# First batch of an induced-attention and leaky-FFN kernel: maxima in three steps, values products moved behind later scores, weight loads spread anew among x

## The chip, the cores and the metric

One core of one Trainium2 chip. The metric is the device time in microseconds of one execution; the kernel before took 1542.71 us, the median of 3 runs.

## What is computed

x is 4 batches of 12480 rows of 128 values, the inducing set is 32 rows of 128, and the FFN has 2048 hidden columns.

```python
def mab(q, kv):
    s = scale * (q @ kv.transpose(0, 2, 1))
    s = s - s.max(-1, keepdims=True)
    a = np.exp(s)
    a /= a.sum(-1, keepdims=True) + 1e-09
    return a @ kv
h = mab(I, x)            # per batch: 32 inducing rows look at all rows of x
y = mab(x, h)            # every row of x looks at the 32 rows of h
...
h = y @ w_in
g = np.maximum(0.01 * h, h)
return (g @ w_out).astype(np.float32)
```

w_in and w_out come as 64-bit floats and are turned to 32-bit on the chip. h of a batch is needed before anything else of that batch can be computed, since the weights that the FFN really uses are h times w_in (tile `hws`).

## The kernel before, in words

Rows of a batch are cut into six groups of 2048 (four blocks of 512, sixteen 128-row slices) and a remainder of 192 rows (group RG). A group comes in as four quarters of 256 KB (tile `xr`).

**First attention, batch 0** (`first_batch`, lines 502 to 597). Nothing can hide it, so it has an order of its own, written out by hand. Per group: `turn` transposes the quarters on PE into PSUM (`xT_ps`, L538) and copies them out on ACT (L544); `scores` multiplies by the inducing rows (`s_ps`, L305); `running` on DVE copies the scores out with their maximum (L317) and spreads it on a diagonal (`rd`, L329), PE adds that up so that every partition has all maxima (`mx_ps`, L334), DVE takes the least of the negated maxima (`nm`, L342 or L345), ACT forms the correction `al` of the older groups (L353) and the exponentials with their sum (L357). `transposed` turns the exponentials on DVE (`ay`, L453), `accumulate` multiplies them with the raw rows on PE (`h_ps`, L425) and adds the result to the running `hacc` times `al` (L441). So the maximum runs on in seven steps, one for each group, and the values products of a group come two rounds later, between the transposes and the scores of a newer group. `sums` (L483) and `normalise` (L496, L498) end it with `hT`.

**Weights.** Eight blocks of 512 KB, four of w_in and four of w_out, each loaded by SP (L179, L185) and converted by `from_double`: one ACT operation (`cv_a`, L131), four DVE operations (`cv_b` L132, `cv_a` L136, `cv_b` L140, `cv_t` L144) and one on POOL (L148). Five loads stand in SP's queue among the quarters of x, behind quarters 2, 6, 10, 14 and 18 (counted from 0); the others follow as buffers come free. Conversion steps (`late`), turns of w_in (`turning`, L233), splits of w_out into a rounded and a remaining part (`splits`, w_hi L202 on ACT, w_lo L203 on POOL) and a small product that keeps PE at work (`keep_ps`, L248) are stepped between the pieces of the first attention by the tables ROUNDS and DRAIN, where "l", "t", "s" and "k" name them. The four w_in blocks are converted first, then the four of w_out.

**From hT on.** The first two tiles of 512 rows take a quick way (`quick`, L739 to L781: q_ps, a_ps, tile A). `expand_weights` makes `hws` in four blocks (product L617, split into two parts L601 and L603). The FFN runs in slots (tile, one of 16 hidden blocks): `ffn_first` makes ph (L821), ghi on ACT (L829) and glo on DVE (L831), and `ffn_second` three output products (L849). The first two tiles share the slots by turns of four. `setup_w12` multiplies turned w_in with w_out (`w_ps`, L259; L263, L265), and `expand_linear` makes from it `m2s` (m_ps, L648), with which a tile ends (L855). `second` is the second attention of the next tiles, `first_scores` and `after_h` the first attention of the next batch, one step at a time among the slots. The main loop (L953) steps each of these lists in a fixed order; every engine carries out its own instructions in the order in which the program issues them.

Of the kernel before, what the change touches and what calls it, by code (L numbers as in the profile page):

```python
# [9 lines left out]
F32 = mybir.dt.float32  # L10
F32R = mybir.dt.float32r
I32 = mybir.dt.int32
# [7 lines left out]
def induced_attention_then_leaky_ffn(  # L20
# [34 lines left out]
    while N - base >= 4 * TOK:  # L55
# [13 lines left out]
    LOADS = [2, 6, 10, 14, 18]  # L69

    ROUNDS = [
        ["", "", "", "", "l"],
        ["l", "l", "", "", "ll", "", ""],
        *[["l", "l", "", "", "ll", "", "", ""]] * 3,
        ["l", "l", "", "", "llt", "", "", ""],
        ["l", "st", "l", "l", "l"],
    ]
    DRAIN = ["l", "", "tk", "l", "l", "", "kk", "", "s"]  # L80

# [36 lines left out]
    def from_double(raw, dst):  # L118
# [7 lines left out]
        n = dst.shape[1]  # L126
# [21 lines left out]
        nc.gpsimd.tensor_tensor(out=dst, in0=a.bitcast(F32), in1=tail, op=ALU.add)  # L148
# [25 lines left out]
    raws = []  # L174

    def load_w_in(c):
        tag, bufs = ("xc", 3) if c < 3 else ("hws", 2)
        raw = sb.tile([P, TOK, 2], I32, tag=tag, name="raw", bufs=bufs)
        nc.sync.dma_start(raw, words(w_in)[:, c * TOK : (c + 1) * TOK, :])  # L179
        return raw  # L180

    def load_w_out(c):
        tag, bufs = ("xc", 3) if c else ("hws", 2)
        raw = sb.tile([P, 4, P, 2], I32, tag=tag, name="raw", bufs=bufs)
        nc.sync.dma_start(  # L185
            raw,
            words(w_out).rearrange("(f p) n t -> p f n t", p=P)[:, 4 * c : 4 * c + 4],
        )
        return raw.rearrange("p f n t -> p (f n) t")

    def setup_w_in():
        for c in range(NF // 4):
            yield from from_double(raws[c], w_in_sb[:, c * TOK : (c + 1) * TOK])
            if c < 3:
                raws.append(load_w_out(c + 1))
            yield

    wraws = []
# [8 lines left out]
    def setup_w_out():  # L207
        for c in range(NF // 4):
            wraw = sb.tile([P, 4, P], F32, tag="xr", name="wraw", bufs=XR)
            wraws.append(wraw)  # L210
            yield from from_double(raws[NF // 4 + c], wraw.rearrange("p f e -> p (f e)"))
            ready.append(c)
            yield

    ready = []

    def parts_of_w_out():
        for c in range(NF // 4):
            while c >= len(ready):
                yield  # L220
            if c:
                yield from idle(3)
            split_w_out(c)
            yield
# [3 lines left out]
    def turn_w_in():  # L228
# [12 lines left out]
        for c in range(NF // 4):  # L241
            copied(turned(c))
            yield
# [7 lines left out]
    def setup_w12():  # L251
        for c in range(NF // 4):
            while c >= len(ready):
                yield
            if c == len(ready) - 1:
                yield from idle(3)
# [245 lines left out]
    def first_batch():  # L502


        order = [*range(RG), RG]
        kinds = [("xr", XR)] * XR + [("ghi", LOOK + 2)] * (LOOK + 2) + [("glo", LOOK + 2)] * (LOOK + 2)
        todo = quarters(0, order)
        for i, (b, g, q) in enumerate(todo):
# [6 lines left out]
            if i in LOADS:  # L515
                c = LOADS.index(i)
                raws.append(load_w_in(c) if c < NF // 4 else load_w_out(0))

        chains, ays = {}, {}
        hacc = None  # L520

        def turn(i, q):
            g = order[i]
# [20 lines left out]
            nc.scalar.copy(  # L544
# [4 lines left out]
        def scores(i):  # L549
            g = order[i]  # L550
            sp = aux_ps("s1_ps")
            for j in range(GROUPS[g][1]):
                columns_product(sp, indT, 0, g, j)
            chains[i] = running(0, g, sp)
            next(chains[i])

        def parts(i):
            return max(1, GROUPS[order[i]][2] // 4) if i < len(order) else 0

        n = len(order)  # L560
        for i in range(n):
            bg = iter(ROUNDS[i])
            for q in range(parts(i)):
                turn(i, q)
                yield next(bg)
            if i >= 1:
                for _ in range(3):
                    next(chains[i - 1])
                yield next(bg)
            if i == n - 1:  # L570
                scores(i)
                yield next(bg)
            if i >= 2:
                hacc = yield from accumulate(0, order[i - 2], hacc, *ays.pop(i - 2), False)
                yield next(bg)
            if i >= 1:
                drain(chains[i - 1])
                ays[i - 1] = transposed(0, order[i - 1])
                yield next(bg)
            if i < n - 1:  # L580
                scores(i)
                yield next(bg)
        bg = iter(DRAIN)
        for _ in range(3):
            next(chains[n - 1])
            yield next(bg)
        hacc = yield from accumulate(0, order[n - 2], hacc, *ays.pop(n - 2), False)
        yield next(bg)
        drain(chains[n - 1])
        ays[n - 1] = transposed(0, order[n - 1])  # L590
        yield next(bg)
        scale = sums(0)
        yield next(bg)
        hacc = yield from accumulate(0, order[n - 1], hacc, *ays.pop(n - 1), False)
        yield next(bg)
        for _ in normalise(0, hacc, scale):
            yield next(bg)
# [424 lines left out]
```

## Time and profile before

| what | value |
| --- | --- |
| median of 3 runs (lowest, highest) | 1542.71 us (1540.13, 1543.12) |
| the profiled execution, its own time | 1541.18 us |
| its span, first to last instruction | 1539.1 us |
| mean granted TensorE clock | 0.992 |
| TensorE busy | 1516.9 us, 99% |
| VectorE busy | 1274.4 us, 83% |
| ScalarE busy | 1005.2 us, 65% |

The profile names the engines PE (TensorE), PEld (its weight loads), DVE (VectorE), ACT (ScalarE), POOL (GpSimd) and SP (SyncE, which issues the DMAs). A row of a timeline has the start in us, the duration, the engine, the line, the operation, what it writes and reads, how often it stands in a row, and in brackets how long the engine was idle before it and what released it. A row of a table by stretches has the stretch and its length, then the busy time of each engine with its number of instructions, then the granted clock (1.00 is full speed), the share of time in which DMA engines were busy, and GB/s. A row of the chain of waits has a start, a duration and the work. Matmuls are pipelined, so the durations of consecutive ones overlap.

### The profile page before, as it was taken

How to read it: one execution, taken by the hardware profiler on the slowest of the kernel's cores; microseconds unless marked ns; L12 is line 12 of the kernel's file. 1: busy time of each engine (PE TensorE's matmuls, PEld its weight loads, DVE VectorE, ACT ScalarE, POOL GpSimd, SP SyncE). 2: the span in 40 equal slices, each digit the busy share in tenths (PEclk: the TensorE clock that was granted, in tenths of full speed). 3: DMA queues.
4: the chain of work that ended last, by engine and by line, in shares of the span. 5: the costliest groups of instructions: out<-in, count | busy, mean ns of one | idle time of the engine just before them, and what ended most of it. 6: DMA issues, size and time to landing. Idle time of an engine off the chain costs nothing.

```text
span 1539.1 us, 22589 instructions
## 1 busy us (share of the span) xinstructions
PE 1516.9 (99%) x7965; PEld 1270.4 (83%) x7965; DVE 1274.4 (83%) x2245; ACT 1005.2 (65%) x1770; POOL 99.0 (6%) x100
## 2 busy tenths in 40 slices
PE   7799999999999999999999999999999999999998
PEld 5588888888888888888888888888888898888887
DVE  6688888887888888888888888887888888888886
ACT  6366666666666666666666666666666666666665
POOL 2110100000101000000001000000111000000000
PEclk9799999999999999999999999999999999999999
DMA  8143334343224354441324246432312112112211
GB/s 277 17 86 59 65 58 90 84 100 69 66 38 86 61 109 93 90 100 22 69 46 90 49 78 129 98 75 50 74 18 51 28 33 49 36 34 42 43 26 21
DMA packets 401313, 104.21 MB, mean 68 GB/s; under 512 B 372368, under 2 KB 374832, under 8 KB 401200
## 3 DMA queue, kind: packets, MB, share of 16 engines
q1 hardware_dynamic: 401152, 102.75, 32.3%
q8 instruction: 63, 1.03, 0.3%
q14 instruction: 50, 0.41, 0.1%
q10 hardware_dynamic: 48, 0.02, 0.0%
HBM read 48.94 MB, written 25.56 MB: 48 GB/s over the span
## 4 chain that ended last, share of the span: by engine, by line
PE 96%; DVE 2%; ACT 1%; DMA 0%; issue 0%; SPq 0%; DVEq 0%
PE po L849 65%; PE ph L821 23%; PE s_ps L305 3%; PE po L855 2%; PE h_ps L425 1%; DMA xr<-in_x_dram 0%; DVE glo L831 0%; PE xT_ps L538 0%; ACT ghi L829 0%; PE a_ps L770 0%; DVE cv_t L144 0%; DVE cv_a L136 0%; PE q_ps L745 0%; ACT xT L544 0%; DVE ay L453 0%
## 5 line engine op out<-in xcount | busy, mean ns | idle before, releaser
L829 ACT ACTIVATE ghi<-ph 128x512 fp32r<-128x512 f32 (+1 forms) x1568 | 929.1, 595 | 492.8 <-PE ph L821 488.0
L831 DVE SCALAR_TENSOR_TENSOR glo<-ph,ghi 128x512 fp32r<-128x512 f32 (+1 forms) x1568 | 1034.1, 678 | 232.0 <-ACT ghi L829 207.7
L821 PE MATMUL ph<-A,hws 128*128 128x512 f32 (+1 forms) x1600 | 607.4, 383 | 5.2 <-DVE hws L603 2.8
L849 PE MATMUL po<-ghi,w_hi 128*128 128x512 f32 (+1 forms) x1568 | 594.2, 379 | 0.0
L849 PE MATMUL po<-glo,w_hi 128*128 128x512 f32 (+1 forms) x1568 | 593.4, 378 | 0.0
L849 PE MATMUL po<-ghi,w_lo 128*128 128x512 f32 (+1 forms) x1568 | 593.4, 378 | 0.0
L821 PEld LDWEIGHTS ph<-A,hws 128*128 128x128 f32 x1600 | 302.5, 189 | 75.8 <-DVE glo L831 21.4
L849 PEld LDWEIGHTS po<-ghi,w_hi 128*128 128x128 f32 x1568 | 297.3, 190 | 43.5 <-issue 0.7
L849 PEld LDWEIGHTS po<-glo,w_hi 128*128 128x128 f32 x1568 | 296.9, 189 | 40.7
L849 PEld LDWEIGHTS po<-ghi,w_lo 128*128 128x128 f32 x1568 | 296.8, 189 | 40.7
L720 POOL TENSOR_TENSOR alo<-aT,ahi 128x512 fp32r<-128x512 f32 x24 | 30.7, 1279 | 669.3 <-ACT ahi L715 666.9
L865 DVE STREAM_TRANSPOSE osb<-po 128x512 f32<-128x512 f32 (+1 forms) x98 | 68.9, 703 | 1.5 <-PE po L855 1.5
L675 POOL TENSOR_TENSOR y<-y,mx 128x512 f32<-128x512 f32 (+1 forms) x27 | 25.3, 936 | 430.4 <-DVE mx L673 430.4
L406 DVE STREAM_TRANSPOSE xT<-xc 128x512 f32<-128x512 f32 x72 | 50.3, 699 | 0.0
L855 PE MATMUL po<-A,m2s 128*128 128x512 f32 (+1 forms) x100 | 43.2, 436 | 0.0
L689 POOL TENSOR_TENSOR y<-y,sm 128x512 f32<-128x512 f32 (+1 forms) x27 | 25.3, 937 | 175.4 <-DVE sm L687 164.2
L425 PEld LDWEIGHTS h_ps<-xr,ay 128*32 128x32 f32 (+1 forms) x784 | 22.7, 112 | 14.2 <-issue 14.2
L425 PE MATMUL h_ps<-xr,ay 128*32 128x128 f32 (+1 forms) x784 | 28.3, 280 | 1.8 <-DVE ay L453 1.8
L305 PE MATMUL s_ps<-xT,indT 128*32 128x512 f32 x192 | 26.4, 622 | 1.1 <-ACT xT L544 1.1
L305 PE MATMUL s_ps<-xT,hT 128*32 128x512 f32 x192 | 25.6, 605 | 0.0
L317 DVE TENSOR_SCALAR_CACHE_REDUCE e<-s_ps 128x512 f32<-128x512 f32 (+1 forms) x28 | 17.1, 609 | 9.3 <-PE s_ps L305 9.2
L855 PEld LDWEIGHTS po<-A,m2s 128*128 128x128 f32 x100 | 18.9, 189 | 2.6
(111 smaller groups left out, 399.8 us busy)
## 6 DMA issues: line engine op xcount, KB each, us to landing
xr<-in_x_dram SPq DMA_DIRECT2D x96, 256.0 KB, 4.4
out_dram<-osb SPq DMA_DIRECT2D x384, 64.0 KB, 2.2
xc<-in_x_dram SPq DMA_DIRECT2D x288, 64.0 KB, 2.7
A<-ahi SPq DMA_DIRECT2D x188, 64.0 KB, 2.0
A<-alo SPq DMA_DIRECT2D x188, 64.0 KB, 2.0
raw<-in_moe_w_in_dram SPq DMA_DIRECT2D x4, 512.0 KB, 6.8
raw<-in_moe_w_out_dram SPq DMA_DIRECT2D x4, 512.0 KB, 7.0
hws<-hwhi SPq DMA_DIRECT2D x24, 64.0 KB, 2.0
```

The costliest lines, as they stand in the source:

```text
L305: nc.tensor.matmul(dst, lhsT, rhs, start=True, stop=True)
L406: nc.vector.transpose(t[:, j, :], blk.rearrange("p n c -> p (n c)"))
L425: nc.tensor.matmul(hp[32 * k : 32 * k + 32, :C], ay[:rows, 4 * q + k, :], xb[:rows, k, :], start=(q == 0), stop=(4 * q + 4 >= K), tile_pos ...
L675: eng.tensor_tensor(out=yv, in0=yv, in1=mx[:rows, :K].unsqueeze(2).broadcast_to([rows, K, M]), op=ALU.subtract,)
L689: eng.tensor_tensor(out=yv, in0=yv, in1=smv.unsqueeze(2).broadcast_to([rows, K, M]), op=ALU.mult)
L720: (eng or nc.gpsimd).tensor_tensor(out=alo[sl], in0=aT.pop((b, g))[: 32 * J, :], in1=ahi[sl].bitcast(F32), op=ALU.subtract,)
L821: nc.tensor.matmul(ph[:, o : o + w], hw[b][1][:, f * P : (f + 1) * P], woven(A4[t][:, o : o + w], t), start=True, stop=True,)
L829: nc.scalar.activation(ghi[:, :n], ph[:, :n], AF.Relu)
L831: nc.vector.scalar_tensor_tensor(out=glo[:, :n], in0=ph[:, :n], scalar=0.0, in1=ghi[:, :n].bitcast(F32), op0=ALU.max, op1=ALU.subtract,)
L849: nc.tensor.matmul(po[:, :n], w[:, f, :], woven(r[:, :n], t), start=(f == 0 and r is ghi and w is w_hi), stop=False)
L855: nc.tensor.matmul(po[:, o : o + w], hw[b][2], woven(a4[:, o : o + w], t, 2), start=False, stop=(o + w == n),)
L865: nc.vector.transpose(osb[:, :n], po[:, :n])
```

## The change

All of it concerns batch 0, the weights and the first two tiles; the code of later batches and the steady slots stays.

- The maximum is taken in three steps: groups 0 to 2, groups 3 and 4, then group 5 with RG. Each step has one `mx_ps` product and one minimum; the values products of a step's groups add up in PSUM (`hpA`, `hpB`, `hpC`), and `hacc` is corrected once for each step. RG comes before the last full group in the order of loads.
- The values products of a group come behind the scores of a later one.
- Weights are loaded in the order w_in 0, w_out 0, w_in 1, w_out 1 and so on, behind quarters 5, 11, 17 of x and the rest behind the last, and converted in that order. The last load waits for the conversion of the fifth block.
- The order of the first attention is written out as one list of calls instead of tables; `l()` is a conversion step. The second quarter is copied on DVE. `keep_ps` is not called any more.
- Uses of a weight block wait, as the program is written out, until the steps that convert it have been issued. In the main loop a conversion step comes in every slot, not every second, and the first slots of the second tile are begun later.

```diff
-    LOADS = [2, 6, 10, 14, 18]
...
+    LOADS = {5: 1, 11: 1, 17: 1, 24: 4}
+    WEIGHTS = [("in", 0), ("out", 0), ("in", 1), ("out", 1), ("in", 2), ("out", 2), ("in", 3), ("out", 3)]
...
+    def convert_weights():
+        for i, (kind, c) in enumerate(WEIGHTS):
+            if kind == "in":
+                yield from from_double(raws[i], lambda: w_in_sb[:, c * TOK : (c + 1) * TOK])
+            else:
+                yield from from_double(raws[i], w_out_part)
+            ready[kind] += 1
+            if i == 4:
+                load_weights()
+            yield
...
         for c in range(NF // 4):
+            while c >= ready["in"]:
+                yield
             copied(turned(c))
             yield
...
+        def peak(g, rd, i):
...
+            nc.vector.tensor_scalar(
+                out=e[:rows, :w], in0=scored.pop(g)[:rows, :w], scalar1=1.0, scalar2=None,
+                op0=ALU.mult, op1=ALU.max, accum_out=rm[:rows],
+            )
...
+            nc.vector.tensor_scalar(
+                out=rd[:, 4 * i : 4 * i + 4], in0=own, scalar1=rm, scalar2=None, op0=ALU.mult,
+                op1=ALU.min, accum_out=any_,
+            )
...
+        turn(3, 0)
+        turn(3, 1)
+        peak(2, rdA, 2)
+        pm = spread(rdA)
+        turn(3, 2)
+        turn(3, 3)
+        nmA, _ = least_of(pm, None)
+        l()
+        exps(0, nmA)
+        scores(3)
+        l()
+        turned(0)
+        hpA = values_ps()
+        values(0, hpA, True, ())
+        exps(1, nmA)
+        peak(3, rdB, 0)
...
+        exps(3, nmB)
+        l()
+        turn(5, 2)
+        turn(RG, 0)
+        turn(5, 3)
+        l()
+        turned(3)
+        exps(4, nmB)
+        l()
+        rdC = peaks(2)
+        scores(5)
+        scores(RG)
+        step(lane["turn"])
+        l()
+        peak(5, rdC, 0)
+        peak(RG, rdC, 1)
+        pm = spread(rdC)
+        hpB = values_ps()
+        values(3, hpB, True, ())
+        turned(4)
+        values(4, hpB, False, range(4))
+        nmC, alC = least_of(pm, nmB)
+        exps(5, nmC)
+        exps(RG, nmC)
...
             for c in range(4):
                 sl = slice(c * TOK, (c + 1) * TOK)
+                while c >= ready["in"]:
+                    yield
                 pw = ps_s.tile([P, TOK], F32, tag="hp", name="hw_ps")
...
-            if u + LOOK < NT * NF:
-                ffn_first(u + LOOK)
+            while begun <= (TURN - 1 if u < LOOK else min(u + LOOK, NT * NF - 1)):
+                ffn_first(begun)
+                begun += 1
             ffn_second(u)
+            step(two)
             if f == NF - 1:
                 stores.append(store(t))
             debt[0] = max(0, debt[0] - 1)
-            if u % 2 == 0:
-                step(late)
+            step(late)
```

Three places show how instructions move. The first is PE in the first attention, at the transposes of the last full group. Before, four quarters (xr_154 to xr_160), maxima, a turn of w_in, the values of group 3 and then the scores:

```order
L538 MATMUL xT_ps<-ident,xr_154 128x128 x4
L538 MATMUL xT_ps<-ident,xr_156 128x128 x4
L538 MATMUL xT_ps<-ident,xr_158 128x128 x4
L538 MATMUL xT_ps<-ident,xr_160 128x128 x4
L334 MATMUL mx_ps<-rd,e_75 128x4
L233 MATMUL winT_ps<-ident,w_in_sb 128x128 x4
L425 MATMUL h_ps<-xr_134,ay 32x128 x4
...
L305 MATMUL s_ps<-xT,indT 32x512 x4
```

Now, with RG's quarter (xr_149) among them:

```order
L528 MATMUL xT_ps<-ident,xr_151 128x128 x4
L572 MATMUL mx_ps<-rd_167,e_75 128x8
L528 MATMUL xT_ps<-ident,xr_153 128x128 x4
L528 MATMUL xT_ps<-ident,xr_155 128x128 x4
L528 MATMUL xT_ps<-ident,xr_149 128x96 x2
L528 MATMUL xT_ps<-ident,xr_157 128x128 x4
L300 MATMUL s_ps<-xT,indT 32x512 x4
L300 MATMUL s_ps<-xTr,indT 32x64 x3
```

The scores stand directly behind the transposes, and the values products of group 3 behind the scores.

The second is ACT at the same place. Before, the four copies of the last full group stand in a row, behind the correction, the exponentials and the conversion of an older round:

```order
L353 ACTIVATE al<-nm 128x1
L357 ACTIVATE e,zg<-e,nm 128x512
L131 ACTIVATE cv_a<-raw 128x512
L544 COPY xT<-xT_ps 128x512 x4
L353 ACTIVATE al<-nm 128x1
```

Now the copies of two quarters of group 4 and two of group 5 come first, then the exponentials of group 3 (e_345) and a conversion, and then the rest of group 5 and RG:

```order
L535 COPY xT<-xT_ps 128x512 x4
L588 ACTIVATE al<-nm 128x1
L598 ACTIVATE e_345,zg<-e_345,nm 128x512
L120 ACTIVATE cv_a<-raw 128x512
L535 COPY xT<-xT_ps 128x512
L535 COPY xTr<-xT_ps 128x192
L535 COPY xT<-xT_ps 128x512
L598 ACTIVATE e_422,zg<-e_422,nm 128x512
```

The last copies moved behind an exponential and a conversion.

The third is DVE in slots of the first two tiles, at the third block of hws (hws <- hw_ps). Before, one conversion (its cv_t here) is left:

```order
L831 SCALAR_TENSOR_TENSOR glo<-ph,ghi 128x512
L144 SCALAR_TENSOR_TENSOR cv_t<-raw,cv_b 128x512
L831 SCALAR_TENSOR_TENSOR glo<-ph,ghi 128x512 x3
L603 SCALAR_TENSOR_TENSOR hws<-hw_ps,hws 64x512
L265 SCALAR_TENSOR_TENSOR w_82<-w_ps,w_82 128x128
```

Now the conversion of w_in's fourth block stands here, one step in each slot:

```order
L121 TENSOR_SCALAR cv_b<-raw 128x512
L763 SCALAR_TENSOR_TENSOR hws<-hw_ps,hws 64x512
L837 TENSOR_TENSOR y<-y,mx 128x512
L993 SCALAR_TENSOR_TENSOR glo<-ph,ghi 128x512
L125 SCALAR_TENSOR_TENSOR cv_a<-cv_a,cv_b 128x512
L993 SCALAR_TENSOR_TENSOR glo<-ph,ghi 128x512
L129 TENSOR_SCALAR cv_b<-cv_a 128x512
L993 SCALAR_TENSOR_TENSOR glo<-ph,ghi 128x512
L133 SCALAR_TENSOR_TENSOR cv_t<-raw,cv_b 128x512
```

Behind its last step (cv_t) the program issues the fourth product of hws on PE, the last turn of w_in, and then ph of slot 12; slot 8's output products stand ahead of them.

More of the change, by code (lines that the diff above doesn't have):

```diff
@@ L205, in split_w_out @@
         )
[L207 to L215, printed above, removed]
     def parts_of_w_out():
         for c in range(NF // 4):
-            while c >= len(ready):
+            while c >= ready["out"]:
                 yield
             if c:
-                yield from idle(3)
+                yield from idle(1)
             split_w_out(c)
@@ L514, in first_batch, with turn @@
             xr[b, g, q] = t
[L515 to L523, printed above, removed]
+            for _ in range(LOADS.get(i, 0)):
+                load_weights()
+        scored, kept, zcols, ays = {}, {}, {}, {}
+        def turn(g, q, on_vector=False):
             _, J, K = GROUPS[g]
@@ L547, in turn, with scores @@
             )
-        def scores(i):
-            g = order[i]
-            sp = aux_ps("s1_ps")
+        def scores(g):
+            scored[g] = sp = aux_ps("s1_ps")
             for j in range(GROUPS[g][1]):
                 columns_product(sp, indT, 0, g, j)
[L554 to L582, printed above, removed]
@@ new lines, in values_ps, with l @@
+        def values_ps():
+            return ps_s.tile([P, TOK], F32, tag="hp", name="h_ps")
+        def l(n=1):
+            for _ in range(n):
+                step(lane["late"])
+        rdA, rdB = peaks(3), peaks(2)
+        for q in range(4):
+            turn(0, q, q == 1)
+        scores(0)
+        turn(1, 0)
+        turn(1, 1)
+        peak(0, rdA, 0)
+        turn(1, 2)
+        turn(1, 3)
+        scores(1)
+        l()
+        turn(2, 0)
+        turn(2, 1)
+        l()
+        peak(1, rdA, 1)
@@ new lines, in first_batch @@
+        l(2)
+        turn(2, 2)
+        turn(2, 3)
+        scores(2)
+        turn(3, 0)
[14 more added lines that the diff above has]
+        peak(3, rdB, 0)
+        turn(4, 0)
+        turned(1)
+        turn(4, 1)
+        values(1, hpA, False, ())
@@ new lines, in first_batch @@
+        exps(2, nmA)
+        l()
+        turn(4, 2)
+        turn(4, 3)
+        turned(2)
+        l()
+        scores(4)
+        values(2, hpA, False, range(4))
+        peak(4, rdB, 1)
+        turn(5, 0)
+        pm = spread(rdB)
+        turn(5, 1)
+        hacc = sb.tile([P, C], F32, tag="hacc", name="hacc", bufs=2)
+        nc.vector.tensor_copy(hacc, hpA[:, :C])
+        nmB, alB = least_of(pm, nmA)
+        exps(3, nmB)
+        l()
+        turn(5, 2)
+        turn(RG, 0)
+        turn(5, 3)
@@ new lines, in first_batch @@
+        zs = added(zs, 3, alB)
+        zs = added(zs, 4)
+        old, hacc = hacc, sb.tile([P, C], F32, tag="hacc", name="hacc", bufs=2)
+        nc.vector.scalar_tensor_tensor(
+            out=hacc, in0=old, scalar=alB, in1=hpB[:, :C], op0=ALU.mult, op1=ALU.add
+        )
+        turned(5)
+        step(lane["turn"])
+        hpC = gen_ps("h_ps")
+        values(5, hpC, True, (2, 3))
+        zs = added(zs, 5, alC)
+        turned(RG)
+        zs = added(zs, RG)
+        sums_of[0] = zs
+        values(RG, hpC, False, (0, 1))
```

202 lines of the change are left out of this document (140 added, 62 removed).

## Prediction

> **What bounds the kernel now.** I read the page first, then the busy time by stage, the granted clock in short windows, the engines' timelines over the first 105 us, and the chain of waits.
>
> ```profile
> PE 1516.9 (99%) x7965; PEld 1270.4 (83%) x7965; DVE 1274.4 (83%) x2245; ACT 1005.2 (65%) x1770; POOL 99.0 (6%) x100
> ...
> PE 96%; DVE 2%; ACT 1%; DMA 0%; issue 0%; SPq 0%; DVEq 0%
> ```
>
> The second line is the chain that ended last: 96% of it is PE. Time can only come from stretches in which PE waits or runs slowly. By stage (time, then busy time of PE, PEld, DVE, ACT, POOL, then clock and DMA):
>
> ```profile
> 0.00:47.76 47.76, 36.86 (x386) 26.41 (x386) 31.47 (x104) 27.29 (x59) 11.56 (x14) 0.93 0.67 225
> 47.76:61.33 13.57, 11.98 (x91) 9.03 (x91) 5.66 (x16) 4.29 (x9) 0.00 (x0) 0.50 0.27 42
> 61.33:81.00 19.67, 16.42 (x88) 12.55 (x87) 15.13 (x25) 10.08 (x20) 3.80 (x3) 1.00 0.08 13
> 81.00:103.05 22.05, 22.00 (x105) 17.15 (x106) 18.68 (x33) 14.07 (x26) 3.60 (x3) 1.00 0.30 56
> 103.05:300.00 196.95, 196.95 (x1023) 163.76 (x1022) 170.35 (x311) 130.04 (x229) 15.11 (x15) 1.00 0.38 75
> ```
>
> From 103.05 us, the end of the first two tiles, PE never waits, and the change alters nothing behind that point. So the question is one number: when does the changed kernel get there? The marks on the way are the first quick product q_ps (47.76), the first output product (61.33), and m_ps (81.00), which waits for the last part of w12.
>
> **The change, part by part.** First, up to q_ps. Rows of PE, then ACT and DVE:
>
> ```profile
> 2.59 6.56 DMA xr<-in_x_dram
> ...
> 10.98 1.93 PE L305 MATMUL s_ps<-xT,indT 128*32 128x512 f32 x8 [0.67 <-ACT xT L544]
> ...
> 12.84 3.68 PE L538 MATMUL xT_ps<-ident,xr 128*128 128x128 f32 x16
> ...
> 17.19 1.07 PE L305 MATMUL s_ps<-xT,indT 128*32 128x512 f32 x8 [0.45 <-ACT xT L544]
> ...
> 22.08 1.97 PE L538 MATMUL xT_ps<-ident,xr 128*128 128x128 f32 x16
> ...
> 24.09 1.08 PE L425 MATMUL h_ps<-xr,ay 128*32 128x128 f32 x32
> ...
> 24.99 1.04 PE L305 MATMUL s_ps<-xT,indT 128*32 128x512 f32 x8
> ...
> 29.90 1.97 PE L538 MATMUL xT_ps<-ident,xr 128*128 128x128 f32 x16
> ...
> 36.64 0.26 PE L305 MATMUL s_ps<-xTr,indT 128*32 128x64 f32 x3
> ```
>
> ```profile
> 20.99 0.74 ACT L357 ACTIVATE e<-e,nm 128x512 f32<-128x512 f32 x1
> 21.70 0.70 ACT L131 ACTIVATE cv_a<-raw 128x512 f32<-128x512 f32 x1
> ...
> 22.77 2.06 ACT L544 COPY xT<-xT_ps 128x512 f32<-128x512 f32 x4 [0.37 <-PE xT_ps L538]
> ```
>
> ```profile
> 22.67 0.65 DVE L317 TENSOR_SCALAR_CACHE_REDUCE e<-s_ps 128x512 f32<-128x512 f32 x1
> ...
> 23.52 0.68 DVE L136 SCALAR_TENSOR_TENSOR cv_a<-cv_a,cv_b 128x512 int32<-128x512 int32 x1
> ...
> 24.24 0.43 DVE L140 TENSOR_SCALAR cv_b<-cv_a 128x512 int32<-128x512 int32 x1
> ...
> 24.73 0.69 DVE L144 SCALAR_TENSOR_TENSOR cv_t<-raw,cv_b 128x512 f32<-128x512 uint32 x1
> ...
> 26.12 0.69 DVE L453 STREAM_TRANSPOSE ay<-e 128x512 f32<-128x512 f32 x1
> ```
>
> The fourth quarter of x landed at 9.15 (first row), behind a weight of 512 KB. Without that weight it lands about 7.0 to 7.5, and the first scores start at 9.1 instead of 10.98. The next four quarters are at half speed (3.68 us), so the second scores start about 15.05 instead of 17.19: 2.1 us ahead.
>
> Then before takes 3.9 us a round (two from 22.08 to 29.90), all of it PE work: transposes 1.8, maxima 0.2, values 0.9, scores 1.0. Between a group's transposes and its scores stand maxima and values, and the copies hide behind these. The new order puts scores straight behind the group's last transposes. Each round pays the copy: a copy starts 0.7 after its transposes do, lasts 0.5 to 0.6, so PE idles 0.85 to 0.95. I laid the new order out by these rows, each engine in its order:
> - scores of group 2 at 18.75 (transposes from 16.0), of group 3 at 22.85;
> - values of group 0 at 25.0: two copies and a cv_a stand on ACT ahead of the first exponential (23.4 to 24.1), and DVE's cv_a, queued ahead of the transpose, waits for ACT too. PE idles 1.2;
> - scores of group 4 at 29.45; last transposes end 33.5;
> - scores of group 5 at 35.95: on ACT al, the exponential of group 3 and a cv_a (0.2+0.7+0.6) stand ahead of the last three copies. PE idles 2.45;
> - scores end 37.1. Before's end at 36.9 (last PE row): the lead is gone.
>
> That is 14.6 us of PE work and 6.5 of waits between 16.0 and 37.1. The tail is shorter than before's 10.9 (36.9 to 47.76): peaks of both last groups 1.35, values of groups 3 and 4 1.8 beside the last minimum and exponentials, DVE's accumulation and transpose 1.3, values 1.2, sums to hT 2.3, waits between them, 8.2 in all. Before's tail also held conversion steps on DVE. **q_ps starts at 45.3: 2.5 us gained.**
>
> Second, from q_ps on. Three of eight weights are converted by then; before had all but one. Five conversions, each four DVE operations (0.34+0.61+0.34+0.6 back to back, 1.9 us), go among the first slots: four more, 7.6 us on DVE.
>
> ```profile
> 47.76 1.92 PE L745 MATMUL q_ps<-hT,xT 128*128 128x32 f32 x8 [0.35 <-ACT hT L498]
> ...
> 56.55 1.22 PE L821 MATMUL ph<-A,hws 128*128 128x512 f32 x2 [1.59 <-DVE A L778]
> ...
> 57.70 1.94 PE L770 MATMUL a_ps<-ident,qy 128*32 128x128 f32 x32
> ...
> 67.22 1.02 PE L617 MATMUL hw_ps<-w_in_sb,hT 128*128 128x512 f32 x2
> ...
> 91.65 1.89 DVE L831 SCALAR_TENSOR_TENSOR glo<-ph,ghi 128x512 fp32r<-128x512 f32 x3 [0.61 <-ACT ghi L829]
> ...
> 77.09 1.28 POOL L148 TENSOR_TENSOR wraw<-cv_a,cv_t 128x512 f32<-128x512 f32 x1 [7.85 <-issue]
> ...
> 81.00 0.49 PE m_ps L648 x2
> ...
> 101.91 0.21 PE ph L821
> ...
> 102.13 0.65 PE po L849 x3
> ...
> 102.78 0.28 PE po L855
> ```
>
> Times from q_ps, the clock halved as in before at that place, and full again at about 16 (before 13.6), once a_ps and the first output have filled a stretch. The first ph comes at 8.8 (56.55 less 47.76; same steps). Then two glo stand on DVE ahead of the second tile's sums, so its a_ps runs 12.65 to 14.55 (before: from 9.94), and the fourth glo ends at 16.5. The fifth glo starts at 20.05, behind the first three output groups, a turned block and the second attention's scores on PE. From it DVE is the bound: eight glo (4.9), six conversion steps (2.9), maximum, difference and one hws (1.9), with 1.0 of holds by POOL (below) to the last step of w_in's fourth block: X = 30.65. The fourth hw_ps waits on PE for X plus POOL's 1.3, and queued behind it are w_in's last turn and ph of slot 12. DVE, waited for till then, now waits for that ph: 4.1 us idle (POOL 1.4, hw 0.9, turn 0.5, ph and copy, ghi). Then four other ACT operations hold ghi 13 for 1.5, and ghi 17 stands behind the last w_hi, which waits for w_out's last block. m_ps comes X plus 15.3, at 45.95. Behind it PE has 16 slots of 0.865 (0.21+0.65), scores 1.2, two linear products: 15.85. **End: 61.8 after q_ps, against 55.3 (103.05 less 47.76): 6.5 us lost.**
>
> Sum: 6.5 less 2.5 is 4.0 us slower. The profiled execution took 1541.18 (span 1539.1), so it becomes 1545.2; the median lies 1.5 above it, and gives 1546.7. A measurement here tells about 0.2%, 3.1 us.
>
> The holds are bounded by these rows:
>
> ```profile
> 38.17 1.79 DVE L144 SCALAR_TENSOR_TENSOR cv_t<-raw,cv_b 128x512 f32<-128x512 uint32 x1
> ...
> 38.14 1.27 POOL L203 TENSOR_TENSOR w_lo<-wraw,w_hi 128x512 fp32r<-128x512 f32 x1 [3.13 <-ACT w_hi L202]
> ```
>
> A conversion step begun while POOL worked took 1.79 instead of 0.69. With POOL's eight conversions and four w_lo in the same order, one to three steps before X can be caught: 0 to 2 us, I take 1.0. The Trainium skill, SBUF — State Buffer, section Who interferes with whom, says that a DVE instruction with two SBUF inputs and a GpSimd instruction that reads SBUF exclude each other. By that rule, the trace agrees, and the difference beside w_lo of the third block would be held too: the 2 us end.
>
> Smaller edits: keep_ps (three small products) and four maxima products go, all on PE in stretches that wait anyway: 0, or up to 1 us of gain where PE is late. One copy on DVE is hidden by DVE's idle start. SP's later loads wait for conversions, but tile 2's blocks come some 3 us ahead of their use.
>
> **The rivals.** The clock decides 4 us either way:
>
> ```profile
> 34.12:37.53 3.41, 2.41 (x47) 1.00 0.00 0
> 37.53:40.94 3.41, 1.57 (x23) 0.99 0.00 0
> ...
> 51.18:54.60 3.42, 3.42 (x41) 0.50 0.68 106
> ...
> 13.65:17.06 3.41, 3.09 (x16) 1.00 1.04 390
> ```
>
> It halved after a stretch of 3.4 us with 1.57 busy, not after one with 2.41; a full one at half clock did not restore it.
>
> *Clock holds into the quick products.* My layout has 1.6 busy in 34.1 to 37.5 and 1.4 in 40.9 to 44.35, near the limit. If it stays full, or drops only between the quick products and the fourth ph, the 6.5 becomes 2.7 to 4.7: 0 to 2 slower, 1543.7. Chance 0.25.
>
> *Clock drops in the gap before group 5's scores.* 2.45 us idle; if a stretch covers it, the tail's products (5 us) run at half speed and q_ps comes at about 49: 7.7 slower, 1550.4. Chance 0.13.
>
> *The first stage keeps pace with the transfers (faster).* Before's last group was on PE from 29.9; with two weights (1.05 MB at 390 GB/s, 2.7 us) fewer ahead, the last quarter lands near 27.4. If copies do not stand behind exponentials as I lay out, its scores end at 29.5, q_ps starts near 37.7, and the gain of 10.1 beats the 6.5: 1539.1, or 1535 with the clock held. It decides once q_ps is before 41.3. Against it: ACT's order is fixed, and each wait follows from it. Chance 0.22.
>
> *A transposing PE stays cold.* In before the clock rose at about 17, after 3.09 us of mostly transposes in 3.41 (last row above; products behind it are twice as fast). The Trainium skill, TensorE: Matmul & The Clock Gate, Part 4, says that transposes do not count as busy for the gate; by that rule, the trace disagrees, since it rose. As a mechanism: twelve more quarters at 0.9 instead of 0.45 cost about 5 us, 1551.7. Chance 0.05.
>
> **How the numbers follow.** My forecast has 0.35: 3 to 5 slower over the hold bounds; 0.07 of that lies within 3.1. Slower: 0.28+0.13+0.05 = 0.46. Same: 0.25+0.07 = 0.32. Faster: 0.22. The range runs from 1536, inside the faster case, to 1551.5, the clock dropped early: about a tenth is left out on each side. The slower cases alone span 1545.8 to 1552.
>
> **What would show it.** Right: q_ps at 44 to 47 with ACT's copies ahead of group 5's scores late; a PE wait of several us at the fourth hw_ps for POOL; m_ps about 46 us behind q_ps; half clock from q_ps on. Wrong: scores ending before 33; m_ps within 35 us of q_ps; PE busy all through the first slots.

## The result and the profile after

The changed kernel takes 1556.12 us (median of 4 runs, 1553.84 to 1557.97), the kernel before 1541.8 us beside it. The ratio is 1.0094, with a 95% interval of 1.0078 to 1.0110: some 14 us slower, where 4.0 were forecast. The profiled execution took 1556.56 us, its span is 1554.4.

Two lines of its page, the busy times and the chain that ended last:

```profile
PE 1517.4 (98%) x7951; PEld 1265.7 (81%) x7951; DVE 1273.9 (82%) x2234; ACT 1003.8 (65%) x1764; POOL 98.9 (6%) x100
...
PE 96%; DVE 1%; ACT 1%; SPq 1%; issue 0%; DMA 0%; POOL 0%; DVEq 0%; ACTq 0%
```

PE is busy for 0.5 us more than before, in a span that is 15.3 us longer: by the records, PE stands idle for nearly all of the difference. By stage (columns as in the table of before: length, busy time of PE, PEld, DVE, ACT, POOL, then clock, DMA share, GB/s; the cuts are the first q_ps, the first output product, m_ps and the end of the first two tiles):

```profile
0.00:48.51 48.51, 34.26 (x367) 23.09 (x367) 22.03 (x79) 22.68 (x48) 4.52 (x9) 0.93 0.60 209
48.51:61.67 13.16, 8.34 (x89) 5.70 (x90) 9.20 (x23) 4.96 (x10) 2.69 (x2) 0.84 0.00 1
61.67:101.75 40.08, 28.58 (x116) 20.67 (x115) 25.68 (x43) 15.68 (x29) 8.89 (x7) 0.76 0.20 37
101.75:118.35 16.60, 16.60 (x84) 12.91 (x83) 13.08 (x23) 10.26 (x19) 2.35 (x2) 1.00 0.37 70
118.35:320.00 201.65, 201.65 (x1045) 167.58 (x1044) 174.82 (x318) 132.96 (x234) 15.18 (x15) 1.00 0.39 75
```

The first two tiles end at 118.4 instead of 103.05: 15.3 us, the whole difference of the spans, and behind them PE is busy all the time, as before. The stage that lost is the third, from the first output product to m_ps: 40.08 us against 19.67, with PE idle for 11.5 of them and the clock at 0.76. The chain of waits names what PE stood behind there (start, duration, work):

```profile
59.22 1.93 PE a_ps L932 x32
...
63.91 1.27 POOL w_in_sb L137
65.23 1.11 PE winT_ps L226 x4
66.34 1.28 PE po L1011 x3
67.62 1.87 PE s_ps L300 x8
69.49 1.58 PE po L1011 x3
72.02 1.89 DVE glo L993 x3
...
85.00 2.08 PE hw_ps L779 x2
...
95.33 1.62 issue
96.95 1.27 POOL wraw L137
98.27 1.99 PE w_ps L254 x8
100.68 1.27 PE po L1011 x3
```

Twice in these rows a step that uses a converted weight block comes right behind POOL's last operation on that block (63.91 to winT_ps, 96.95 to w_ps). Ahead of the fourth hw_ps the chain follows DMA issues of SP instead (L286), but the timelines of POOL and PE show the same picture there:

```profile
83.69 1.26 POOL L137 TENSOR_TENSOR w_in_sb<-cv_a,cv_t 128x512 f32<-128x512 f32 x1 [4.08 <-DVE cv_t L133]
```

```profile
85.00 2.08 PE L779 MATMUL hw_ps<-w_in_sb,hT 128*128 128x512 f32 x2 [7.02 <-POOL w_in_sb L137]
```

Which of the two it waits for, POOL or SP, e12 below decides. The waits of PE in that part of the program, added up by pair (us in total, times, longest):

```profile
PE hw_ps L779 <- POOL w_in_sb L137: 7.0, 1, 7.0
PE a_ps L932 <- DVE qy L925: 3.0, 2, 2.5
PE w_ps L254 <- POOL wraw L137: 2.3, 1, 2.3
PE winT_ps L226 <- POOL w_in_sb L137: 2.1, 1, 2.1
```

7.0, 2.3 and 2.1 are 11.4 us. That is one theory, T: **PE stands in program order behind uses of weight blocks whose conversion is late.** The second, C: **half clock, which the waits bring about, is most of the loss.** In stretches of 3.41 us counted from where the clock first fell:

```profile
30.16:33.57 3.41, 3.41 (x57) 2.66 (x50) 1.71 (x8) 1.02 (x2) 1.16 (x1) 1.00 0.54 199
33.57:36.98 3.41, 1.16 (x14) 0.61 (x15) 1.75 (x4) 3.41 (x10) 0.00 (x0) 1.00 0.01 2
36.98:40.39 3.41, 2.87 (x28) 1.68 (x21) 2.74 (x14) 0.66 (x2) 1.27 (x1) 0.50 0.00 0
40.39:43.80 3.41, 3.41 (x65) 2.83 (x58) 0.74 (x7) 1.33 (x5) 0.00 (x0) 0.50 0.00 0
43.80:47.21 3.41, 2.17 (x42) 1.65 (x42) 1.97 (x8) 1.18 (x2) 0.00 (x0) 1.00 0.02 5
...
54.03:57.44 3.41, 0.92 (x3) 0.49 (x3) 1.85 (x3) 2.51 (x6) 0.47 (x1) 1.00 0.01 2
...
77.90:81.31 3.41, 0.08 (x1) 0.00 (x0) 3.32 (x5) 1.84 (x4) 1.26 (x1) 1.00 0.09 13
...
94.95:98.36 3.41, 1.11 (x6) 0.65 (x4) 3.34 (x8) 0.25 (x2) 1.26 (x1) 1.00 0.02 4
```

Read the first number behind the length (PE busy) and the third from the end (clock). Each of the four stretches with 0.08 to 1.16 us busy is followed by half clock; one with 2.17 is not. In all, half clock lasts 30.7 us here, in four pieces, where the kernel before had 20.5 in one (40.88 to 61.36). The third theory, R: **DVE, which now converts five blocks behind hT instead of one, is the bound**, and waits would come back in another place if these were taken away.

### The profile page after: what moved, and what is told of

Same layout as the page of the kernel before. It is cut to its first block, busy times and chain, and to the rows that moved or that the text cites. A ratio compares the mean times of both kernels' runs of the same rounds, so it can differ in the third digit from the quotient of the medians.

```text
span 1554.4 us, 22547 instructions
## 1 busy us (share of the span) xinstructions
PE 1517.4 (98%) x7951; PEld 1265.7 (81%) x7951; DVE 1273.9 (82%) x2234; ACT 1003.8 (65%) x1764; POOL 98.9 (6%) x100
## 4 chain that ended last, share of the span: by engine, by line
PE 96%; DVE 1%; ACT 1%; SPq 1%; issue 0%; DMA 0%; POOL 0%; DVEq 0%; ACTq 0%
PE po L1011 65%; PE ph L983 23%; PE s_ps L300 3%; PE po L1017 2%; PE h_ps L420 1%; SPq L286 1%; ACT xT L535 1%; PE h_ps L629 1%; PE xT_ps L528 0%; DMA xr<-in_x_dram 0%; PE w_ps L254 0%; DVE glo L993 0%; ACT ghi L991 0%; PE mx_ps L329 0%; PE hw_ps L786 0%
## 5 line engine op out<-in xcount | busy, mean ns | idle before, releaser
L420 PEld LDWEIGHTS h_ps<-xr,ay 128*32 128x32 f32 (+1 forms) x588 | 16.9, 110 | 11.8 <-issue 11.8
L535 ACT COPY xT<-xT_ps 128x512 f32<-128x512 f32 x23 | 12.6, 590 | 16.6 <-PE xT_ps L528 16.5
L832 DVE STREAM_TRANSPOSE y<-s_ps 128x512 f32<-128x512 f32 (+1 forms) x28 | 17.9, 639 | 3.9 <-PE s_ps L300 3.9
```

The costliest lines, as they stand in the source:

```text
L420: nc.tensor.matmul(hp[32 * k : 32 * k + 32, :C], ay[:rows, 4 * q + k, :], xb[:rows, k, :], start=(q == 0), stop=(4 * q + 4 >= K), tile_pos ...
L535: copy(t[:, 4 * q : 4 * q + nk], pt[:, : nk * rows].rearrange("p (k j r) -> p k j r", k=nk, r=32),)
```

## The experiments

All against the kernel before on the same chip. "q_ps" is the start of the first quick product, "rest" the time from there to the end of the first two tiles, both read from PE's timeline of the profiled execution. Before: 47.76 and 55.3; changed: 48.51 and 69.9.

| kernel | median us | ratio to before, 95% | q_ps | rest |
| --- | --- | --- | --- | --- |
| changed | 1556.12 | 1.0078 to 1.0110 | 48.51 | 69.9 |
| e1 products in the gaps | 1549.33 | 1.0032 to 1.0066 | 47.30 | 65.7 |
| e2 copies first | 1558.09 | 1.0093 to 1.0123 | 48.69 | 69.6 |
| e3 later uses | 1545.33 | 1.0014 to 1.0033 | 49.69 | 58.9 |
| e12 only the fourth hw_ps later | 1554.09 | 1.0062 to 1.0095 | 48.45 | 67.4 |
| e4 two more conversions before hT | 1549.71 | 1.0037 to 1.0067 | 51.81 | 59.6 |
| e5 addition on DVE | 1551.96 | 1.0055 to 1.0085 | 47.53 | 66.3 |
| e6 later uses and products | 1541.22 | 0.9992 to 1.0011 | 47.51 | 56.5 |
| e7 later uses, short conversions | 1540.70 | 0.9984 to 1.0003 | 47.69 | 55.0 |
| e8 interleaved first attention | 1554.01 | 1.0063 to 1.0097 | 44.97 | 71.2 |
| e9 later uses, products, interleaved | 1540.04 | 0.9983 to 1.0000 | 45.06 | 56.5 |
| e10 the same, addition on DVE | 1542.67 | 1.0001 to 1.0019 | 45.92 | 58.7 |
| e11 before, with products | 1539.88 | 0.9980 to 0.9998 | 47.59 | 55.1 |

**Later uses (e3).** Only PE's uses of late blocks move back in program order:

```diff
         for c in range(NF // 4):
             while c >= ready["in"]:
                 yield
+            if c >= 2:
+                yield from idle((2, 4)[c - 2])
             copied(turned(c))
...
             if c == ready["out"] - 1:
-                yield from idle(1)
+                yield from idle(2)
...
-                yield from idle(3 if c else 1)
+                yield from idle((1, 3, 6, 3)[c])
```

> The changed kernel with only PE's use of late weight blocks moved back in program order: the fourth hw_ps three slots later, the third and fourth turn of w_in 2 and 4 slots later, each w12 product one slot more behind its split. The conversions stay where they are. Theory T: the waits of 2.1, 7.0 and 2.3 us for POOL go, the clock keeps up between 65 and 102 us, the end of the first two tiles comes 9 to 12 us earlier, the whole 9 to 12 us faster than the changed kernel (about 1545). Theory R: DVE stays as late, the waits appear again as waits of ph and po for glo, 3 us faster or less. Theory C without T: some 4 us.

Measured: 1545.33, 10.8 us faster than the changed kernel, and the rest takes 58.9 instead of 69.9. PE's waits from q_ps on in its trace:

```profile
PE ph L985 <- DVE glo L995: 2.9, 1, 2.9
PE a_ps L934 <- DVE qy L927: 2.3, 1, 2.3
```

No wait for POOL is left, and of the 11.4 us only 2.9 came back as a wait of ph for DVE's glo. The same conversions run on the same engines; only what stands behind them in PE's order is another. The late ones come earlier by that: POOL's step on w_in's fourth block starts at 82.05 instead of 83.69, and the one on w_out's last block at 88.10 instead of 96.95. In the changed kernel PE's wait held them up too, since DVE, with the steps of w_out's last block still to do, stood idle for 5.48 us, till 89.09, for the ph queued behind the fourth hw_ps. That is T, with R in the 2.9.

**Only the fourth hw_ps later (e12).**

```diff
-                yield from idle(3 if c else 1)
+                yield from idle((1, 3, 6, 3)[c])
```

> The changed kernel with only the fourth hw_ps issued three slots later; the turns of w_in and the products of w12 stay. Nothing is left out. Theory T with the waits as single prices: the 7.0 us wait goes or shrinks under 1 us, the waits of the third turn (2.1) and of the last w12 product (2.3) stay; 6 to 7.5 us faster than the changed kernel (about 1549.5), so that the other two places account for 3 to 4.5 of the 10.8 us. If the fourth turn, which needs the same block, then waits in its place: 1 to 3 us faster only (about 1554).

Measured: 1554.09, only 2.0 us faster; the second expectation holds. In PE's timeline the wait has moved, whole, to the fourth turn, which needs the same block:

```profile
85.63 1.11 PE L226 MATMUL winT_ps<-ident,w_in_sb 128*128 128x128 f32 x4 [7.01 <-POOL w_in_sb L137]
...
91.91 1.02 PE L779 MATMUL hw_ps<-w_in_sb,hT 128*128 128x512 f32 x2
```

7.02 became 7.01, and the turn now pays it. So the price belongs to the block and to whichever use of it comes first, not to the product that the profile names, and it is POOL's result that is waited for, not SP's issues.

**Products in the gaps (e1).** A product that nobody reads, so that PE does not fall idle:

```diff
+    def keep(n):
+        for _ in range(n):
+            pt = aux_ps("keep_ps")
+            nc.tensor.matmul(pt[:, : 2 * P], ident, w_in_sb[:, : 2 * P], start=True, stop=True)
```

> The changed kernel with 34 products that nobody reads (128x256, of a converted block of w_in) put where PE waits: 4 ahead of group 5's scores, 4 ahead of the first ph, 4 ahead of the second tile's a_ps, 4 ahead of the third turn of w_in, 14 ahead of the fourth hw_ps, 4 ahead of the last product of w12. Nothing is left out. Theory C (the loss is mostly half clock in the gaps: 37 to 44, 57 to 71, 82 to 88, 99 to 102 us): the clock stays up, the end of the first two tiles comes 8 to 10 us earlier than 118.4, the whole 8 to 10 us faster than the changed kernel (about 1547). Theory T (PE stands behind POOL's results of late conversions): the waits of 2.1, 7.0 and 2.3 us stay as PE idle or as these products, and the gain is only what ran at half speed on the chain, 3 to 5 us (about 1552). Theory R (DVE with the moved conversions is the bound): 3 us or less.

Measured: 1549.33, 6.8 us faster, between what C (8 to 10) and T (3 to 5) expected. The clock stayed at 1.00 up to q_ps and fell once behind it, from 49 to 56 us. The 14 products ahead of the fourth hw_ps do not shorten what it stands behind, they fill it: it starts 35.05 us behind q_ps instead of 36.49.

From e3 to **later uses and products (e6)** the same kind of products goes into what idle time is left (a line of `keep` at five places, one of them this):

```diff
+                if begun == 12:
+                    keep(6)
                 ffn_first(begun)
```

> The kernel with the later uses of weights (1545.3 us) and, besides, 22 products that nobody reads where PE still idles: 4 ahead of group 5's scores, 4 ahead of hT, 4 ahead of the first ph, 4 ahead of the second tile's a_ps, 6 ahead of the ph of slot 12. Nothing is left out. Theory C, in its smaller form (half clock costs what it lengthens on the chain): the clock stays at 1.00 up to the end of the first two tiles, 3 to 4 us faster than without these products (about 1542). If the stretches at half clock lie beside DVE's work: 1 us or less (1544.5 to 1545.5).

Measured: 1541.22, 4.1 us below e3 and level with the kernel before. Its clock is 1.00 from q_ps to the end of the first two tiles:

```profile
47.51:103.91 56.40, 52.97 (x314) 39.49 (x315) 48.22 (x87) 31.02 (x58) 13.91 (x11) 1.00 0.27 50
```

The products thus bring 4.1 us where the waits are gone and 6.8 where they are there. As the clock stays full in e6, I read that as about the price of half clock; no run takes the clock apart from the rest that the products change. The two effects overlap: 10.8 and 6.8 are more than the 14.9 us between the changed kernel and e6.

**Short conversions (e7).** On top of e3, the four DVE steps of the last four conversions are left out:

```diff
+        if short:
+            for _ in range(3):
+                yield
+            nc.gpsimd.tensor_tensor(out=dst(), in0=a.bitcast(F32), in1=a.bitcast(F32), op=ALU.add)
+            return
```

> The kernel with the later uses of weights (1545.3 us), with the four DVE steps of the last four conversions left out (the blocks then hold other numbers; ACT's and POOL's steps stay), so 16 DVE steps of 0.34 to 0.6 us, 7.6 us, less among the first slots. Theory R (what is left of the loss is DVE's load behind h): the 2.9 us wait of ph for glo goes and the end of the first two tiles comes 4 to 6 us earlier than 108.6, the whole 1540 to 1541.5, level with the kernel before or faster. If DVE's load is hidden: 1 us or less.

Measured: 1540.70, 4.6 us below e3. Of the 7.6 us that DVE was spared, 4.6 came back as time: the rest is 3.9 shorter, and q_ps, ahead of the edit, comes 2.0 earlier in this execution, in which the clock stayed up there. The wait of ph for glo shrinks from 2.9 to 1.5, where R expected it to go. So R holds for what is left once the waits are gone: DVE's load behind hT is on the path. e6 and e7 both take the rest to about before's; whether their gains add was not tried.

**Two more conversions before hT (e4).** 
```diff
         zs = added(zs, 4)
+        l(4)
...
         zs = added(zs, RG)
+        l(4)
```

> The changed kernel with two more conversions (eight DVE steps, 3.8 us by the rows) put on DVE in the tail before hT, so that five instead of three of eight weights are converted by q_ps, three instead of five left behind it. Theory T: w_in's fourth block is ready eight slots earlier, the 7.0 us wait at the fourth hw_ps goes, and the two smaller ones shrink; q_ps comes 0 to 3 us later; net 8 to 10 us faster (about 1547). Theory R: DVE has 3.8 us less behind h, and its tail before h is 0 to 3 later: about 1 to 4 us faster (about 1553).

Measured: 1549.71, 6.4 us faster; less than T expected, and for a reason that the expectation had too small: q_ps comes 3.3 us later, because the steps stand on DVE between the sums and the transposes for which PE waits:

```profile
43.90 0.43 DVE L129 TENSOR_SCALAR cv_b<-cv_a 128x512 int32<-128x512 int32 x1
44.36 0.69 DVE L133 SCALAR_TENSOR_TENSOR cv_t<-raw,cv_b 128x512 f32<-128x512 uint32 x1
44.97 0.34 DVE L729 SCALAR_TENSOR_TENSOR hacc<-hacc,al,h_ps 128x128 f32<-128x128 f32 x1
45.22 0.71 DVE L619 STREAM_TRANSPOSE ay<-e 128x512 f32<-128x512 f32 x1
...
45.98 2.31 PE L629 MATMUL h_ps<-xr,ay 128*32 128x128 f32 x36 [2.59 <-DVE ay L619]
```

The rest is then 59.6, nearly e3's: three late conversions instead of five also take the 7.0 us wait away. Waits for POOL of 2.7 us at a turn and 1.7 at a w12 product are left.

**Addition on DVE (e5).**

```diff
-        nc.gpsimd.tensor_tensor(out=dst(), in0=a.bitcast(F32), in1=tail, op=ALU.add)
+        nc.vector.tensor_tensor(out=dst(), in0=a.bitcast(F32), in1=tail, op=ALU.add)
```

> The changed kernel with the last step of each conversion, the addition, on DVE instead of POOL. Nothing is left out. If DVE steps are held by POOL as the 1.79 us and 1.27 us rows suggest: the held rows among the first slots (cv_t 0.84, cv_b 1.27, the difference 1.41; about 1.9 us above their other rows) go back to 0.69, 0.42 and 0.69, the fourth hw_ps no longer waits the 1.3 us of POOL behind the last DVE step, and DVE has 0.6 us more for each of five late blocks: fourth hw_ps 1.5 to 2.5 us earlier, the whole 1 to 3 us faster than the changed kernel (about 1554). If the holds have nothing to do with POOL: 1 to 3 us slower (about 1558).

Measured: 1551.96, 4.2 us faster, more than expected; the fourth hw_ps starts 33.55 behind q_ps instead of 36.49, with a wait of 5.07 instead of 7.02. The held rows of the changed kernel's DVE, and POOL's beside them:

```profile
76.33 1.28 POOL L137 TENSOR_TENSOR wraw<-cv_a,cv_t 128x512 f32<-128x512 f32 x1 [6.94 <-PE ph L983]
78.34 1.26 POOL L206 TENSOR_TENSOR w_lo<-wraw,w_hi 128x512 fp32r<-128x512 f32 x1 [0.73 <-ACT w_hi L205]
```

```profile
75.35 0.84 DVE L133 SCALAR_TENSOR_TENSOR cv_t<-raw,cv_b 128x512 f32<-128x512 uint32 x1
...
76.72 1.27 DVE L121 TENSOR_SCALAR cv_b<-raw 128x512 int32<-128x512 int32 x1
...
78.74 1.41 DVE L837 TENSOR_TENSOR y<-y,mx 128x512 f32<-128x512 f32 x1
```

and the same rows in e5, where POOL has only w_lo left:

```profile
74.96 1.34 POOL L206 TENSOR_TENSOR w_lo<-wraw,w_hi 128x512 fp32r<-128x512 f32 x1 [6.07 <-ACT w_hi L205]
```

```profile
72.68 0.82 DVE L133 SCALAR_TENSOR_TENSOR cv_t<-raw,cv_b 128x512 f32<-128x512 uint32 x1
...
74.75 0.41 DVE L121 TENSOR_SCALAR cv_b<-raw 128x512 int32<-128x512 int32 x1
...
75.90 0.94 DVE L837 TENSOR_TENSOR y<-y,mx 128x512 f32<-128x512 f32 x1
```

cv_b falls from 1.27 to 0.41, with POOL's addition gone from beside it, and the difference from 1.41 to 0.94; it ends about 0.5 us behind the end of w_lo both times (80.15 behind 79.60, 76.84 behind 76.30). So these two holds come from POOL. The third row that the expectation named, cv_t, does not go back: 0.84 and 0.82, both times while POOL stands idle, so what lengthens it stays open. Of the 4.2 us about 1.0 lies ahead of q_ps (47.53 instead of 48.51). The row of the difference agrees with the Trainium skill, SBUF — State Buffer, section Who interferes with whom, by which a DVE instruction with two SBUF inputs and a GpSimd instruction that reads SBUF exclude each other; y minus mx reads two.

**Copies first (e2).** 
```diff
-        exps(3, nmB)
-        l()
         turn(5, 2)
         turn(RG, 0)
         turn(5, 3)
+        exps(3, nmB)
+        l()
```

> The changed kernel with the exponential of group 3 and one conversion step issued behind the last quarter's turn, so that ACT copies group 5 and RG first. If the place of these two ACT operations ahead of the copies made the gap before group 5's scores: scores(5) start 1.5 to 2 us earlier than 36.4, the clock stays at 1.00 through the tail, q_ps 3 to 5 us earlier than 48.5, and the whole 3 to 5 us faster than the changed kernel (about 1552). Rival: the exponential and the correction that come later hold the values of group 3 and the next minimum for as long, q_ps within 1 us, the whole within 1 us of the changed kernel.

Measured: 1558.09, no faster. q_ps starts at 48.69, within 1 us, as the rival said; the time is 2.0 us above the changed kernel's, more than its 1 us, but the two intervals overlap. Scores of group 5 do start earlier, at 34.81, and the next wait takes the gain:

```profile
34.81 1.06 PE L300 MATMUL s_ps<-xT,indT 128*32 128x512 f32 x8 [1.01 <-ACT xT L535]
...
36.09 0.69 DVE L125 SCALAR_TENSOR_TENSOR cv_a<-cv_a,cv_b 128x512 int32<-128x512 int32 x1 [3.21 <-ACT cv_a L120]
36.70 0.70 DVE L619 STREAM_TRANSPOSE ay<-e 128x512 f32<-128x512 f32 x1
...
40.08 0.42 PE L572 MATMUL mx_ps<-rd,e 128*128 128x8 f32 x2 [3.51 <-DVE rd L560]
```

DVE's conversion step cv_a waits 3.21 us for ACT's cv_a, which now comes behind the copies and the exponential. The transpose of group 3 and the maxima stand behind it on DVE, and the product of the maxima waits 3.51 us for them.

**Interleaved first attention (e8).** Each group's scores behind the first quarter of the next group:

```diff
         turn(2, 2)
         turn(2, 3)
+        turn(3, 0)
         scores(2)
-        turn(3, 0)
         turn(3, 1)
```

> The changed kernel with another order in the first attention alone: each group's scores stand behind the first quarter of the next group's transposes instead of straight behind its own, and the values of group 3 ahead of group 5's scores. If the waits for copies (0.67, 0.68, 0.83, 0.73, 0.72 and 2.25 us ahead of the scores, 0.96 ahead of the values) made the first stage no faster than before's: they go, scores(5) start 4 to 5 us earlier than 36.4, the clock may hold in the tail, q_ps at 43 to 45 instead of 48.5, the whole 4 to 5 us faster than the changed kernel (about 1551.5). If the transfers of x set the pace there: the scores wait for them instead, 1 us or less.

Measured: 1554.01, 2.1 us faster, half of what was expected. The waits for copies do go (0.2 us is left), scores of group 5 start at 34.07 and q_ps at 44.97, 3.5 us earlier; but the waits for x among the transposes grow from 0.8 to 3.3 us, the product of the maxima waits 1.8 for DVE instead of 0.5, and the rest takes 71.2 instead of 69.9, with a clock of 0.78 there instead of 0.83. The first lines of PE's waits in that stage and behind it:

```profile
PE hw_ps L779 <- POOL w_in_sb L137: 7.0, 1, 7.0
PE xT_ps L528 <- DMA xr<-in_x_dram: 3.3, 4, 1.0
```

**Together (e9 and e10), and the kernel before with products (e11).** e9 is e3, e8 and the products, 4 of them at another place:

```diff
-        keep(4)
         scores(5)
...
+        keep(4, gen_ps)
         pm = spread(rdC)
```

> Three edits that each made the changed kernel faster, together: later uses of weights, scores behind the next group's first transposes, and 22 products that nobody reads where PE idles (4 now ahead of the last maxima product instead of ahead of group 5's scores). Nothing is left out. If their gains are separate places of one chain (later uses 10.8, products 4.1, interleaved scores 2.1 to 3.5 us at q_ps): 1538 to 1539.5 us, 2 to 3.5 faster than the kernel before. If the earlier q_ps is given back behind it, since the conversions on DVE then set the end: 1541 to 1541.5, level with the kernel without interleaving.

Measured: 1540.04, 1.2 us below e6. In the profiled execution the earlier q_ps is kept (45.06, and the rest 56.5 as in e6), in the medians half of it. It is level with the kernel before: the interval ends at 1.0000. It is level, too, with e11 below, the kernel before with such products (1539.88): even repaired, the new order gains nothing over the old one.

e10 is e9 with the edit of e5:

> The same with the last addition of each conversion on DVE instead of POOL. Nothing is left out. With the waits for POOL gone by the later uses, there remain the holds (1.9 us gained) against five additions of 0.6 us (3.0 us lost) on DVE among the first slots: if DVE's load sets the end of the first two tiles, 0 to 1.5 us slower than without this edit; if what gained 4.2 us in the changed kernel were the holds alone, 2 us faster.

Measured: 1542.67, 2.6 us slower than e9, worse than the 0 to 1.5 expected. By R, five additions on DVE cost more than the holds give back; but q_ps is 0.9 later as well, a_ps waits 1.95 us for DVE, and the clock falls once behind that wait, from 51 to 55 us, so the 2.6 need not be DVE's load alone.

e11 adds to the kernel before:

```diff
-    DRAIN = ["l", "", "tk", "l", "l", "", "kk", "", "s"]
+    DRAIN = ["l", "", "tkkkk", "l", "l", "", "kk", "", "s"]
...
+        keep(4)
         ffn_first(0)
...
+                if u == 5:
+                    keep(6)
                 ffn_first(u + LOOK)
```

> The kernel before with 14 products that nobody reads where PE idles: 4 ahead of the last full group's values products, 4 ahead of the first ph, 6 ahead of the ph that waits 2.8 us for hws. Nothing is left out. If half clock in a gap costs by itself, whatever the order of work: the half-clock stretch from 47.8 to about 61 us gets shorter, 1.5 to 3 us faster than the kernel before (about 1539). If the products only take the place of waits, within 1 us of it.

Measured: 1539.88, 1.7 us faster than the kernel before, in the expected range. The half-clock stretch does get shorter, 13.7 us (44.21 to 57.86) instead of 20.5 (40.88 to 61.36), but q_ps and the rest are each only 0.2 us shorter in this execution, whose own time, 1540.64, is 0.5 below that of the one profiled before. So where the 1.7 us of the median come from stays open.

## Why the prediction was wrong

The sign and the place were right, the size was not: 4.0 us forecast, 15.3 in the profiled span, and the median lies 4.6 us above the range's upper end, 1551.5. By its own steps:

- **The order of the first attention.** Scores of groups 2 to 4 laid out at 18.75, 22.85 and 29.45 came at 18.88, 23.07 and 29.96, the values of group 0 at 25.09 (25.0), group 5's scores at 36.40 (35.95) behind a wait of 2.25 (2.45) for ACT's copies. Right, within about half a microsecond.
- **"q_ps starts at 45.3: 2.5 us gained." This step failed: 48.51.** The tail was sized with full clock at 8.2 us; it took 10.5 (from 38.0). What happened is the rival of the clock dropping in the gap before group 5's scores, which had 0.13 and said 49. The stretch from 33.57 had 1.16 busy, and the values of groups 3 and 4 took 3.64 us at half clock (1.8 laid out). It is partly chance: with the same gap of 2.25 us the clock fell in the changed kernel, e3, e5 and e12, and stayed in e4 and e7. The stretch that holds the gap had 1.16 us busy in the changed kernel, e5 and e12 and 1.51 in e3, against 1.55 in e4 and 1.76 in e7: where the gap falls between the edges differs by run. e1, with the clock held, has q_ps 16.3 us behind group 4's scores instead of 18.55: about 2.2 us are the clock's. Even that rival's 1550.4 lies 5.7 us below what was measured, so the clock in the tail is not the larger part.
- **"The fifth glo starts at 20.05" (from q_ps). This step failed: 23.5.** It counted the third turn of w_in as PE work alone. That turn waits 2.07 us for POOL, and the products behind it ran at half clock, which had held up to 57.44 and so fell later than forecast. The fourth glo, laid out to end at 16.5, ended at 14.7; from there to the fifth it took 8.8 us instead of 3.55: 5.2 lost.
- **"1.0 of holds by POOL". Too small: 1.6** (cv_b 0.85 and the difference 0.73 above their free rows), within the 0 to 2 that the text gave; e5 took 1.3 of it back. From the fifth glo to the last step of w_in's fourth block 11.6 us instead of 10.6.
- **"The fourth hw_ps waits on PE for X plus POOL's 1.3", with the last turn and ph of slot 12 queued behind it.** Right, and the largest wait; e12 shows that queue, e3 what it costs. **"m_ps comes X plus 15.3" failed: 18.1**, because the product after the wait runs at half clock (2.08 instead of 1.02), DVE's idle time behind it is 5.48 us instead of 4.1, and the last product of w12 waits 2.30 for POOL: of w_out's last block the sum had ACT's w_hi, not PE's product queued behind it.
- **End behind m_ps:** 15.85 forecast, 16.6 measured.

Together: 3.2 us up to q_ps, then −1.8, +5.2, +1.0, +2.8 and +0.8, 11.2 in all over the forecast of 4.0. From q_ps on, what was missing is of one kind: of three PE steps queued ahead of need behind a late block, the sum priced one; and each such wait was priced as a wait alone, without the half clock behind it. The two waits that it left out are 2.07 and 2.30 us, 4.4 of the 11.2, and ahead of q_ps the clock took about 2.2; how the rest divides between half clock and DVE's lateness no run measures. e3's 10.8 us is the price of all three waits and of what hangs on them, the forecast one at the fourth hw_ps among them, and e6's 4.1 comes on top. What may be left to gain over e6 is DVE's load: sparing it brought 4.6 us on top of e3 (e7), and on top of e6 it was not tried.

Of the other rivals, the first stage keeping pace with the transfers did not come about, since ACT's fixed order made the waits as laid out; e8 shows that even without them q_ps comes at 44.97, far from the 37.7. A transposing PE that stays cold did not come about either: group 1's scores ran in 1.07 us, at full clock, behind transposes, and in e5 group 0's scores took 1.06 us at 9.02, with little but transposes on PE before them.

## What to carry to other kernels

Where program order is queue order, ask of every step that is moved later who is queued behind its *first* user on each in-order engine, and list all users of the result, since delaying only one of them moves the wait to the next. Price a TensorE wait of some 2 us and more with the half clock that it can bring for several microseconds (the gap of 2.25 us did in four executions and did not in two), and try both orders: uses pushed back by a few slots took 10.8 us off here with no operation changed. A gain in an early stage that is bound by a chain of engines (copies, exponentials, maxima) is kept only if the next link in the chain is early as well.

## What was not expected of the hardware

- The clock moved on a fixed grid: in the changed kernel it fell at 36.98, 57.44, 81.31 and 98.36 us, 6, 7 and 5 times 3.41 us apart. The Trainium skill, TensorE: Matmul & The Clock Gate, Part 1, says that the window of about 3.4 us runs free and does not reset when a kernel starts; this trace agrees, and in e3 an edge lies at 39.35 us, 2.37 from one here. The same part of the Trainium skill says that the clock falls after an idle window; the measurement differs, since here windows with up to 1.16 us busy were enough, and 1.57 in the kernel before. Busy time alone does not decide either: a stretch with 1.55 (e4, 35.83 to 39.24) kept full clock, one with 2.34 (e1, 45.74 to 49.15) lost it.
- At half clock, a grid stretch with 2.87 us busy did not bring the full clock back, one that was full (40.39 to 43.80) did. A full one need not: in the kernel before (51.18 to 54.60) and in e1 (49.15 to 52.56) full stretches of q_ps and a_ps did not bring it back.
- POOL's operation lengthens a conversion step of one SBUF input and integer type too (cv_b 1.27 us beside the addition, 0.41 in e5, where that is gone), not only steps with two inputs.
